# Two-layer segment-recurrent transformer on one core: the last 64 rows of the weight products as column pairs, with tiles numbered by heads

## The chip, the core and the metric

The kernel runs on one core of a Trainium2 chip. The metric is the time of one execution on the device, in microseconds. The kernel before takes 1576.67 us, the median of three runs (1576.35 to 1577.01).

## The reference, cut to what matters

Two kinds of layer alternate, twice: attention with a recurrent memory (A), and a gated feed-forward layer (B). Each is applied to a layer norm of x and added to x.

```python
scale = Dh ** (-0.5)
for s in range(n_seg):                       # 64 segments of 32 rows
    xs = x[:, s * seg_len:(s + 1) * seg_len, :]
    h = jnp.concatenate([mem, xs], axis=1)   # 8 memory rows + 32 rows, 448 wide
    q = jnp.einsum('btd,dhe->bhte', h, Wq)   # 16 heads of 256
    k = jnp.einsum('btd,dhe->bhte', h, Wk)
    v = jnp.einsum('btd,dhe->bhte', h, Wv)
    scores = jnp.einsum('bhqe,bhke->bhqk', q, k) * scale
    scores = jnp.where(mask[None, None], scores, -1000000000.0)
    p = _softmax(scores, axis=-1)
    o = jnp.einsum('bhqk,bhke->bhqe', p, v)
    o = jnp.einsum('bhte,hed->btd', o, Wo)
    mem = o[:, :M, :]                        # the next segment's memory
    outs.append(o[:, M:, :])
# B: h = relu(x @ W_gate) * (x @ W_up); x + h @ W_down
x = x + A(_layernorm(x)); x = x + B(_layernorm(x))
x = x + A(_layernorm(x)); x = x + B(_layernorm(x))
```

## The kernel before

**What is computed in which form.** The weights are multiplied first. For each head, A = Wq Wk^T (448 x 448) and B = Wv Wo (448 x 448); the scores are then h A h^T and the output is P h B. A_sb and B_sb stay on the chip for the whole run.

**Preparation (lines 289 to 435).** A loop over p = 0 to 7 makes A for two heads at a time. `load_nat` (L302) loads 512 columns of Wq and of Wk: 384 rows in one DMA, the last 64 rows in a second, and into the free half of the fourth chunk a third DMA brings 64 rows again (of Wq, or of Wv beside Wk). All of these, and first of all the rows of x (xp, L168), are issued by SyncE. `flips` (L323) turns them on TensorE with `tr` (L151), 8 transposes for each half of 256 columns, and `share` (L316) copies each result out of PSUM on VectorE or ScalarE, by a planned balance of the two. Then 8 slots (kd = 0 to 3 for the four chunks of rows, eo = 0, 1 for the two heads) multiply query rows by key rows: two matmuls of 384 columns into `aps`, and two of 64 columns into `mx_ps`. For kd = 3, the last 64 rows, the query rows stand twice, in both halves of the 128 outputs, and two copies for each head take either half. Between the slots the transposes of the next pair are placed. A second loop makes B the same way from Wv and Wo; the last 64 rows of Wv, collected in v3, are multiplied there as column pairs: two heads at a time, each in 64 columns of the array, with `tile_position` (0, 0) and (0, 64).

**Numbering.** A tile is a chunk of 128 of a head's 448 columns. A half hf holds 8 heads, and 28 tiles: tile 8 kd + 4 eo + p4 for the three full chunks, 24 + p4 for the last columns of two heads together.

**The steps (`step`, L712).** 68 steps follow; step g works on one segment of the first A layer and, from g = 4 to 63, on one of the second (60 steps with two chains; four at either end have one). In each step and half, `project` (L621) multiplies h by the tiles in banks of six (0, 6, 12, 18; and 24 with four), into PSUM. `copies` (L628) evicts each bank to TQ, where the layout is by segment part, kd and head. The 64 last rows of a tile need only half the array's rows, so `project_early` (L608) runs them ahead, two banks at a time, one on the upper and one on the lower half of the rows; EARLY (L43) says which banks go together: 0 with 6 and 12 with 18. Then `scores` (L740) takes 128 columns of TQ for each kd as weights, in the order KD = (0, 1, 3, 2): memory rows (Sm) with the first three, own rows (Sx) with the first three, then both with the last. The softmax runs on VectorE and ScalarE, and the output projection (ox, o) on TensorE.

**What sets the order.** TensorE runs its instructions in the order of the program (`in_order`, L80), in the steps VectorE and ScalarE too (`InOrder`, L93). In the preparation the order on VectorE, ScalarE, GpSimd and SyncE is what the scheduler makes of the dependencies; each of these engines then runs its list strictly in order. SyncE's DMAs use eight completion slots in turn, and a DMA that takes a slot again waits for the one that had it.

Of the kernel before, what the change touches and what calls it, by code (L numbers as in the profile page):

```python
# [8 lines left out]
BF = mybir.dt.bfloat16  # L9
# [6 lines left out]
DM = 448  # L16
# [26 lines left out]
EARLY = (((0, 6), (12, 18)), ((0, 6), (12, 18)))  # L43
# [5 lines left out]


def upper(hf, t):

    return any(b <= t < b + 6 for _, b in EARLY[hf])

# [6 lines left out]
def build_kernel(ctx, tc, A_x, A_mem0, A_Wq, A_Wk, A_Wv, A_Wo, B_W_gate, B_W_up, B_W_down, out,  # L61
# [89 lines left out]
    def tr(out, src, idn):  # L151
        in_order(nc.tensor.transpose(out, src, idn))  # L152
        passed(out, 56)
# [14 lines left out]
    nc.sync.dma_start(xp[1][:], x_dram[0:128])  # L168
# [120 lines left out]
    with tc.tile_pool(name="pre", bufs=6) as pre:  # L289
# [3 lines left out]
        nats = []  # L293
        for i in range(6):
            t = pre.tile([P, 4, 512], BF, name=f"nat{i}", bufs=1)
            nats.append(t)
        nc.gpsimd.memset(A_sb[64:128, 3, :, 24:NT, :], 0.0)
        for t in TQ + TZ + PX + PM + YB:
            nc.gpsimd.memset(t[:], 0.0)
        nn = [0]  # L300

        def load_nat(src, p, eng):  # L302
            t = nats[nn[0] % 6]
            nn[0] += 1
            cols = slice(512 * p, 512 * (p + 1))
            eng.dma_start(t[:, 0:3, :], src[0:384, cols].rearrange("(k p) n -> p k n", p=P))
            if src is Wv:
                return t
            eng.dma_start(t[0:64, 3, :], src[384:448, cols])
            eng.dma_start(t[64:128, 3, :], (Wq if src is Wq else Wv)[384:448, cols])  # L310
            return t
# [11 lines left out]
        def flips(src, p, name):  # L323
            nat = load_nat(src, p, nc.sync)
            o = pre.tile([P, 4, 512], BF, tag="tT", name=name, bufs=4)

            def half(e2):
                tp = bank([P, 2, 512], BF, "tpw")
                n = 3 if src is Wv else 4
                for kd in range(n):  # L330
                    for e in range(2):
                        tr(tp[:, e, kd * 128:(kd + 1) * 128],
                           nat[:, kd, (2 * e2 + e) * 128:(2 * e2 + e + 1) * 128], ident[:])
                n = DM if src is Wk else 128 * n
                share(o[:, 2 * e2:2 * e2 + 2, 0:n], tp[:, :, 0:n], 2 * n, (0.6, 0.82))
                if src is Wk:
                    share(v3[:, p, 2 * e2:2 * e2 + 2, :], tp[:, :, DM:512], 128, (0.6, 0.82))

            return o, [lambda: half(0), lambda: half(1)]

        def queue(p):
            if p < NP:
                qT, a = flips(Wq, p, "qT")
                kT, b = flips(Wk, p, "kT")
                return (qT, kT), a + b
            if p == NP:
                return flips(Wv, 0, "vT")
            return None, []
# [13 lines left out]
        keep_warm(8)  # L362
# [5 lines left out]

        ready, todo = queue(0)
        for k, u in enumerate(todo):  # L370
            if k == 2:
                keep_warm(4)
            u()
        for p in range(NP):
            hf, p4 = divmod(p, 4)
            qT, kT = ready
            ready, todo = queue(p + 1)
            mx_ps = bank([P, 4, 128], F32, "mxw")
            for kd in range(4):
                for eo in range(2):  # L380
                    aps = bank([P, 3, 128], F32, "aps")
                    for t in range(2):
                        e = 2 * eo + t
                        mm(aps[:, :, :], qT[:, e, kd * 128:(kd + 1) * 128],
                           kT[:, e, 0:384], start=(t == 0), stop=(t == 1))
                    for t in range(2):
                        e = 2 * eo + t
                        mm(mx_ps[:, kd, eo * 64:eo * 64 + 64], qT[:, e, kd * 128:(kd + 1) * 128],
                           kT[:, e, 384:448], start=(t == 0), stop=(t == 1))
                    t0 = eo * 4 + p4  # L390
                    if kd < 3:
                        share(A_sb[:, kd, hf, t0:t0 + 17:8, :], aps[:], 384, (1.28, 0.85))
                    else:
                        up = [t for t in range(3) if upper(hf, t0 + 8 * t)]
                        for rows, ts in ((slice(64, 128), up), (slice(0, 64), [t for t in range(3) if t not in up])):
                            if ts:
                                d = ts[1] - ts[0] if len(ts) > 1 else 1
                                share(A_sb[rows, 3, hf, t0 + 8 * ts[0]:t0 + 8 * ts[-1] + 1:8 * d, :],
                                      aps[rows, ts[0]:ts[-1] + 1:d, :], 128 * len(ts), (1.28, 0.85))
                    if todo and 2 * kd + eo in (0, 2, 4, 5):  # L400
                        todo.pop(0)()
            share(A_sb[:, 0:3, hf, 24 + p4, :], mx_ps[:, 0:3, :], 384, (1.28, 0.85))
            share(A_sb[0:64, 3, hf, 24 + p4, :], mx_ps[0:64, 3, :], 128, (1.28, 0.85))
            if p >= 5:
                load_wo(p - 5)
            if p == 1:
                xn0 = normed(row_stats(xp[1]))
            if p == 2:
                first_rows(xn0)

        for p in range(NP):
            hf, p4 = divmod(p, 4)
            vT = ready
            ready, todo = flips(Wv, p + 1, "vT") if p + 1 < NP else (None, [])
            wo = wos.pop(0)
            for eo in range(2):
                for kd in range(3):
                    bps = bank([P, 512], F32, "bps")
                    for t in range(2):
                        e = 2 * eo + t  # L420
                        mm(bps[:, 0:DM], vT[:, e, kd * 128:(kd + 1) * 128], wo[:, e, :],
                           start=(t == 0), stop=(t == 1))
                    share(B_sb[:, hf, tidx(kd, eo, p4), 0:DM], bps[:, 0:DM], DM, (1.28, 0.85))
                    if kd == 1 and todo:
                        todo.pop(0)()
            bps = bank([P, 512], F32, "bps")
            for t in range(2):
                for eo in range(2):
                    e = 2 * eo + t
                    mm(bps[64 * eo:64 * eo + 64, 0:DM], v3[:, p, e, :], wo[:, e, :],  # L430
                       start=(t == 0), stop=(t == 1), tile_position=(0, 64 * eo))
            share(B_sb[:, hf, 24 + p4, 0:DM], bps[:, 0:DM], DM, (1.28, 0.85))
            if p + 3 < NP:
                load_wo(p + 3)
            if p >= 3:
                next_piece()
                next_piece()
# [170 lines left out]
    def project_early(hf, chains, hb, j, pairs=(0, 1)):  # L608

        n = L * len(chains)  # L610
        pre = {}
        for pair in [EARLY[hf][i] for i in pairs]:
            for i0 in pair:
                pre[i0] = bank([P, 512], F32, "prj", hold=True)
            for i in range(6):
                for i0, rows in zip(pair, (slice(0, 64), slice(64, 128))):
                    mm(pre[i0][:, i * n:(i + 1) * n], A_sb[rows, 3, hf, i0 + i, :],
                       moving(hb, j, 3, chains, rows), start=(i == 0), stop=False, skip_group_check=True)
        return pre

    def project(hf, chains, hb, j, banks, pre={}, busy=False, first=None, inside=None):  # L621

        n = L * len(chains)
        for i0, k in banks:
            ps = pre[i0] if i0 in pre else bank([P, 512], F32, "prj")
            two = len(chains) == 2

            def copies(eng, rows, T):  # L628
                T = T.rearrange("p g (t q) -> p t g q", q=16)
                if two:  # L630
                    evac(eng, T, ps[rows, 0:k * n].rearrange("p (t g q) -> p t g q", t=k, q=16))
                    return
                c = chains[0]
                src = ps[rows, 0:k * n].rearrange("p (t w) -> p t w", t=k)
                x, m = (0, SEG) if c == 0 else (MEM, 0)
                evac(eng, T[:, :, 2, MEM * c:MEM * c + MEM], src[:, :, m:m + MEM])
                evac(eng, T[:, :, 3 * c:3 * c + 2, :],
                     src[:, :, x:x + SEG].rearrange("p t (g q) -> p t g q", q=16))
# [12 lines left out]
            if i0 < 24:  # L651
                T = TQ[hf][:].rearrange("p g u w -> p g (u w)")[:, :, 16 * i0:16 * (i0 + k)]
                copies(act if (i0 != 6 if busy and hf else i0 % 12) else dve, slice(0, P), T)
            else:
                copies(act if busy else dve, slice(0, 64), TZ[hf][0:64, :, 0:64])
                copies(act, slice(64, 128), TZ[hf][64:128, :, 64:128])
# [464 lines left out]
```

## Time and profile before

| what | value |
|---|---|
| median of three runs | 1576.67 us (1576.35 to 1577.01) |
| profiled execution | 1574.71 us, span 1572.9 us |
| TensorE busy in the span | 1559.8 us |
| VectorE, ScalarE, GpSimd busy | 1125.3, 744.0, 78.1 us |
| start to the first aps matmul | 9.38 us |
| first loop of the preparation | 9.38 to 48.04 us |
| second loop | 48.04 to 75.63 us |
| bytes moved by DMA | 33.21 MB, nearly all in the first three of 40 slices |

A row of the profile's groups or of its timeline names the line, the engine, the operation, what it writes and reads with shapes, how often, and its duration; in square brackets stands the idle time of the engine just before it and what ended that. Line 102 is the wrapper through which VectorE and ScalarE are called, lines 144 and 152 are the helpers for matmuls and transposes, so instructions are told apart by their tiles. PEld is TensorE's load of weights, which overlaps its matmuls. A table by stages shows for each stretch its length, then for each engine the busy time and the number of instructions, the granted clock of TensorE, the DMA engines' busy share and GB/s.

### The profile page before, as it was taken

The numbers are of one execution on the slowest core, as the hardware profiler recorded it, in microseconds if no ns is written. First come the engines' busy times: TensorE is split into PE (matmuls) and PEld (weight loads), VectorE is DVE, ScalarE is ACT, GpSimd is POOL, SyncE is SP. The second block draws the span as 40 slices with busy tenths as digits, with TensorE's granted clock in tenths as the row PEclk, the third lists the DMA queues.
The fourth block names the chain that finished last, engine by engine and source line by source line (L and its number), as shares of the span: only waits on it lengthen the run. The fifth ranks groups of instructions, "written<-read, shape, count | busy, mean of one in ns | idle before, by whom it ended". The sixth has DMA issues, their size and how long they took to land.

```text
span 1572.9 us, 89355 instructions
## 1 busy us (share of the span) xinstructions
PE 1559.8 (99%) x40988; PEld 1446.1 (92%) x40988; DVE 1125.3 (72%) x3689; ACT 744.0 (47%) x2088; POOL 78.1 (5%) x174
## 2 busy tenths in 40 slices
PE   9999999999999999999999999999999999999998
PEld 6698999999999999999999999999999999999897
DVE  7766777777777777777777777777777777777765
ACT  5754444454444444544444445444444444444443
POOL 3200000000000000000000000000000000000000
PEclk9999999999999999999999999999999999999999
DMA  8630000000000000000000000000000000000000
GB/s 242 201 85 9 8 10 9 8 5 10 9 9 9 10 9 7 7 10 9 10 9 10 10 5 8 10 10 9 10 9 10 4 10 10 9 8 7 6 7 9
DMA packets 28233, 33.21 MB, mean 21 GB/s; under 512 B 4168, under 2 KB 26960, under 8 KB 27856
## 3 DMA queue, kind: packets, MB, share of 16 engines
q1 hardware_dynamic: 26608, 23.76, 5.4%
q8 instruction: 320, 5.24, 1.4%
q0 software_dynamic: 1088, 3.68, 0.7%
q14 instruction: 57, 0.47, 0.1%
q10 hardware_dynamic: 160, 0.06, 0.0%
HBM read 23.70 MB, written 1.84 MB: 16 GB/s over the span
## 4 chain that ended last, share of the span: by engine, by line
PE 98%; DVE 1%; issue 0%; DMA 0%; SPq 0%; ACT 0%; POOLq 0%; POOL 0%; ACTq 0%; DVEq 0%
PE prj L144 32%; PE ox L144 25%; PE gps L144 6%; PE ups L144 6%; PE dps L144 5%; PE o L144 5%; PE y L144 4%; PE Sx L144 3%; PE pps L152 2%; PE bps L144 1%; PE aps L144 1%; PE Sm L144 1%; PE tpw L152 1%; PE ya L144 1%; PE yb L144 1%; PE kps L152 1%
## 5 line engine op out<-in xcount | busy, mean ns | idle before, releaser
L144 PE MATMUL prj<-hT,A_sb 128*128 128x80 bf16 (+3 forms) x15232 | 553.9, 199 | 1.0 <-DVE se L102 0.6
L144 PEld LDWEIGHTS <-A_sb 128*128 128x128 bf16 (+1 forms) x15232 | 507.3, 99 | 23.3 <-issue 1.9
L144 PEld LDWEIGHTS <-B_sb 128*128 128x128 bf16 (+1 forms) x15008 | 489.5, 103 | 14.3 <-issue 1.2
L144 PE MATMUL ox<-Y,B_sb 128*128 128x80 bf16 (+2 forms) x11256 | 443.5, 200 | 1.0 <-issue 0.8
L102 ACT CAST TQ<-prj 128x480 bf16<-128x480 f32 (+1 forms) x380 | 184.1, 496 | 116.3 <-PE prj L144 110.5
L102 DVE CAST Y<-y 128x256 bf16<-128x256 f32 x376 | 151.2, 456 | 36.5 <-PE y L144 36.2
L102 ACT CAST Y<-y 128x512 bf16<-128x512 f32 (+2 forms) x392 | 137.1, 419 | 62.4 <-PE y L144 62.3
L102 ACT ACTIVATE se<-se 128x160 f32<-128x160 f32 (+2 forms) x270 | 81.5, 302 | 140.7 <-DVE se L102 135.4
L102 DVE CAST TQ<-prj 128x480 bf16<-128x480 f32 (+1 forms) x228 | 128.4, 572 | 9.0 <-PE prj L144 8.5
L144 PE MATMUL gps<-xT,Wg_sb 128*128 128x128 bf16 (+3 forms) x1904 | 128.6, 215 | 0.0
L144 PEld LDWEIGHTS <-Wu_sb 128*128 128x128 bf16 (+1 forms) x1904 | 104.9, 97 | 5.7 <-issue 0.2
L144 PEld LDWEIGHTS <-hk 40*128 40x128 bf16 (+1 forms) x1950 | 98.9, 96 | 9.8 <-issue 2.7
L144 PE MATMUL ups<-xT,Wu_sb 128*128 128x128 bf16 (+3 forms) x1632 | 106.8, 216 | 0.5 <-DVE xT L102 0.5
L144 PEld LDWEIGHTS <-Wg_sb 128*128 128x128 bf16 (+1 forms) x1904 | 106.7, 97 | 0.5 <-issue 0.5
L102 ACT COPY os<-o 64x16 f32<-64x16 f32 (+3 forms) x134 | 25.5, 190 | 172.3 <-PE o L144 170.8
L102 ACT CAST TZ<-prj 64x320 bf16<-64x320 f32 (+2 forms) x264 | 96.9, 377 | 17.1 <-DVE TZ L102 13.6
L102 DVE SCALAR_TENSOR_TENSOR hh<-gps,ut 128x512 bf16<-128x512 f32 (+2 forms) x136 | 78.0, 594 | 34.6 <-ACT ut L102 21.8
L144 PE MATMUL dps<-Wd_sb,hh 128*128 128x448 bf16 (+1 forms) x504 | 93.3, 342 | 0.8 <-DVE hh L102 0.8
L102 DVE TENSOR_REDUCE ssum<-se 128x4 f32<-128x160 f32 (+2 forms) x270 | 72.7, 269 | 24.1 <-ACT se L102 24.0
L102 ACT COPY PT<-pps 128x256 bf16<-128x256 bf16 (+1 forms) x136 | 46.5, 343 | 91.0 <-PE pps L152 90.9
L144 PEld LDWEIGHTS <-TQ 128*128 128x128 bf16 x1938 | 85.9, 97 | 1.6 <-ACT TQ L102 0.8
L144 PE MATMUL y<-PT,hk 40*128 40x256 bf16 (+1 forms) x1280 | 86.3, 248 | 0.7 <-ACT Y L102 0.6
(127 smaller groups left out, 1901.6 us busy)
## 6 DMA issues: line engine op xcount, KB each, us to landing
wo<-in_A_Wo_dram POOLq DMA_DIRECT2D x8, 448.0 KB, 5.1
nat<-in_A_Wq_dram SPq DMA_DIRECT2D x8, 384.0 KB, 4.9
nat<-in_A_Wk_dram SPq DMA_DIRECT2D x8, 384.0 KB, 4.8
nat<-in_A_Wv_dram SPq DMA_DIRECT2D x8, 384.0 KB, 4.7
xa<-in_A_x_dram SPq DMA_DIRECT2D x32, 56.0 KB, 2.2
xa<-xp SPq DMA_DIRECT2D x32, 56.0 KB, 1.9
xp<-in_A_x_dram SPq DMA_DIRECT2D x30, 56.0 KB, 2.7
out_dram<-xa SPq DMA_DIRECT2D x30, 56.0 KB, 2.5
```

Of the source, the lines that this page charges most:

```text
L102: r = f(*a, **k)
L144: in_order(nc.tensor.matmul(out, lhsT, rhs, **k))
L152: in_order(nc.tensor.transpose(out, src, idn))
```

## The change

What it does:

- The last 64 rows of Wq and of Wk are loaded into the two halves of one tile (natl), turned together in 4 transposes, and multiplied as column pairs (`by_heads`, `last_rows`): two heads at a time, 64 rows each, 448 columns. The chunk kd = 3 leaves the loop of slots, which has 6 slots a pair. The last rows of Wv are loaded for two pairs of heads at a time and turned in the second loop.
- `last_rows` and `last_out` stand at the end of an even pair and at the start of an odd one, so that two groups are adjacent.
- The first pair's loads are split by heads (256 columns each) and issued by SyncE (Wq) and ScalarE (Wk), ahead of everything else; the first loads go at the top of the program. The load of xp moves into the loop, behind the loads of the second pair.
- The first pair's second head is turned inside the loop; the junk matmuls that keep TensorE busy (`keep_warm`) are 7, 2 and 2 instead of 8 and 4.
- Tiles are numbered by heads: tile 3 (4 eo + p4) + kd. EARLY pairs bank 0 with 12 and 6 with 18, and `copies` writes TQ with one dimension more.

The core of the diff:

```diff
-EARLY = (((0, 6), (12, 18)), ((0, 6), (12, 18)))
+EARLY = ((0, 12), (6, 18))
...
-    nc.sync.dma_start(xp[1][:], x_dram[0:128])
+    prepare = ExitStack()
+    pre = prepare.enter_context(tc.tile_pool(name="pre", bufs=6))
+    nats = [pre.tile([P, 3, 512], BF, name=f"nat{i}", bufs=1) for i in range(6)]
+    nats3 = [pre.tile([P, 512], BF, name=f"natl{i}", bufs=1) for i in range(3)]
...
+    for e in range(2):
+        cols = slice(256 * e, 256 * e + 256)
+        for i, (eng, src) in enumerate(((nc.sync, Wq), (nc.scalar, Wk))):
+            eng.dma_start(nats[i][:, :, cols], rows3(src, cols))
+            if e == 0:
+                eng.dma_start(nats3[0][FR[i], :], src[384:448, 0:512])
...
+        def flip(nat, e2, dst):
+            tp = bank([P, 2, 512], BF, "tpw")
+            for kd in range(3):
+                for e in range(2):
+                    tr(tp[:, e, kd * 128:(kd + 1) * 128],
+                       nat[:, kd, (2 * e2 + e) * 128:(2 * e2 + e + 1) * 128], ident[:])
+            share(dst, tp[:, :, 0:384], 768, (0.6, 0.82))
+
+        def flip_last(nat, dst):
+            tp = bank([P, 4, 128], BF, "tpl")
+            for e in range(4):
+                tr(tp[:, e, :], nat[:, e * 128:e * 128 + 128], ident[:])
+            share(dst, tp[:].rearrange("p e (i d) -> p e i d", i=2), 512, (0.6, 0.82))
...
-        keep_warm(8)
+        keep_warm(7)
...
+        def by_heads(ps, a, b, n):
+            for t in range(2):
+                for eo in range(2):
+                    mm(ps[FR[eo], 0:n], a(2 * eo + t), b(2 * eo + t), start=(t == 0), stop=(t == 1),
+                       tile_position=(0, 64 * eo))
+
+        def last_rows(qk, hf, p4):
+
+            ps = bank([P, DM], F32, "apl")
+            by_heads(ps, lambda e: qk[:, e, 0, 384:DM], lambda e: qk[:, e, 1, :], DM)
+            for eo in range(2):
+                t0 = 3 * (eo * 4 + p4)
+                share(A_sb[FR[eo], 3, hf, t0:t0 + 3, :], ps[FR[eo], 0:384], 384, (1.28, 0.85))
+            for eo in range(2):
+                share(A_sb[FR[eo], 3, hf, 24 + p4, 64 * eo:64 * eo + 64], ps[FR[eo], 384:DM], 64, (1.28, 0.85))
+
         ready, todo = queue(0)
-        for k, u in enumerate(todo):
-            if k == 2:
-                keep_warm(4)
-            u()
+        for k in range(3):
+            todo.pop(0)()
+            if k < 2:
+                keep_warm(2)
         for p in range(NP):
             hf, p4 = divmod(p, 4)
-            qT, kT = ready
-            ready, todo = queue(p + 1)
-            mx_ps = bank([P, 4, 128], F32, "mxw")
-            for kd in range(4):
-                for eo in range(2):
+            qk = ready
+            ready, us = queue(p + 1)
+            todo += us
+            if p == 0:
+                nc.sync.dma_start(xp[1][:], x_dram[0:128])
+            if p % 2:
+                last_rows(qk, hf, p4)
+            mx_ps = bank([P, 3, 128], F32, "mxw")
+            for eo in range(2):
+                t0 = 3 * (eo * 4 + p4)
+                for kd in range(3):
...
-                    if kd < 3:
-                        share(A_sb[:, kd, hf, t0:t0 + 17:8, :], aps[:], 384, (1.28, 0.85))
...
+                    share(A_sb[:, kd, hf, t0:t0 + 3, :], aps[:], 384, (1.28, 0.85))
+                    if todo:
                         todo.pop(0)()
...
+            while todo:
+                todo.pop(0)()
+            if p % 2 == 0:
+                last_rows(qk, hf, p4)
...
-                T = T.rearrange("p g (t q) -> p t g q", q=16)
+                l = T.shape[1]
                 if two:
-                    evac(eng, T, ps[rows, 0:k * n].rearrange("p (t g q) -> p t g q", t=k, q=16))
+                    evac(eng, T, ps[rows, 0:k * n].rearrange("p (l t g q) -> p l t g q", l=l, g=5, q=16))
...
-                T = TQ[hf][:].rearrange("p g u w -> p g (u w)")[:, :, 16 * i0:16 * (i0 + k)]
+                T = TQ[hf][:].rearrange("p g u w -> p g (u w)").rearrange("p g (t m q) -> p m t g q", t=3, q=16)
+                T = T[:, i0 // 3:i0 // 3 + 2]
```

The last two lines select for a bank the two heads i0 / 3 and i0 / 3 + 1, with all three kd each, and write them to the places that they had in TQ before. Loading, turning and multiplying the same rows gives the same A and B as before.

More of the change, by code (lines that the diff above doesn't have):

```diff
@@ L48 @@
 HALF = (slice(0, DM // 2), slice(DM // 2, DM))
-def upper(hf, t):
-    return any(b <= t < b + 6 for _, b in EARLY[hf])
 def tidx(kd, eo, p4):
@@ L166, in block, with rows3 @@
         return slice(TB * i, TB * i + TB)
-    nc.sync.dma_start(xp[1][:], x_dram[0:128])
+    prepare = ExitStack()
+    pre = prepare.enter_context(tc.tile_pool(name="pre", bufs=6))
+    nats = [pre.tile([P, 3, 512], BF, name=f"nat{i}", bufs=1) for i in range(6)]
+    nats3 = [pre.tile([P, 512], BF, name=f"natl{i}", bufs=1) for i in range(3)]
+    def rows3(src, cols):
+        return src[0:384, cols].rearrange("(k p) n -> p k n", p=P)
+    for e in range(2):
[4 more added lines that the diff above has]
+                eng.dma_start(nats3[0][FR[i], :], src[384:448, 0:512])
     still = glob.tile([P, 512], BF, name="still")
@@ L286, in set_mem @@
         dve.tensor_copy(mem_of(g, cs)[:, 0:src.shape[1]], src)
-    with tc.tile_pool(name="pre", bufs=6) as pre:
+    with prepare:
         mem0_n = pre.tile([MEM, 512], BF, name="mem0_n", bufs=1)
@@ L292, in build_kernel, with load_nat, load_last @@
         nc.gpsimd.dma_start(mem0_n[:, DM:512], mem0[:, 384:DM])
[L293 to L297, printed above, removed]
+        for e in range(2):
+            nc.gpsimd.memset(A_sb[FR[e], 3, :, 24:NT, 64 - 64 * e:128 - 64 * e], 0.0)
         for t in TQ + TZ + PX + PM + YB:
             nc.gpsimd.memset(t[:], 0.0)
-        nn = [0]
-        def load_nat(src, p, eng):
+        nn, n3 = [2], [1]
+        def load_nat(src, p):
             t = nats[nn[0] % 6]
             nn[0] += 1
[L305 to L310, printed above, removed]
+            nc.sync.dma_start(t[:], rows3(src, slice(512 * p, 512 * p + 512)))
+            return t
+        def load_last(parts):
+            t = nats3[n3[0] % 3]
+            n3[0] += 1
+            for r, (src, p) in zip(FR, parts):
+                nc.sync.dma_start(t[r, :], src[384:448, 512 * p:512 * p + 512])
             return t
@@ L321, in share @@
             evac(eng, dst, src)
[L323 to L339, printed above, removed]
+        def flip(nat, e2, dst):
+            tp = bank([P, 2, 512], BF, "tpw")
+            for kd in range(3):
+                for e in range(2):
+                    tr(tp[:, e, kd * 128:(kd + 1) * 128],
+                       nat[:, kd, (2 * e2 + e) * 128:(2 * e2 + e + 1) * 128], ident[:])
+            share(dst, tp[:, :, 0:384], 768, (0.6, 0.82))
@@ L341, in queue @@
+        def flip_last(nat, dst):
[3 more added lines that the diff above has]
+            share(dst, tp[:].rearrange("p e (i d) -> p e i d", i=2), 512, (0.6, 0.82))
         def queue(p):
             if p < NP:
[L343 to L347, printed above, removed]
@@ L348, in queue @@
-            return None, []
+                nat = nats[0:2] if p == 0 else [load_nat(src, p) for src in (Wq, Wk)]
+                last = nats3[0] if p == 0 else load_last(((Wq, p), (Wk, p)))
+                qk = pre.tile([P, 4, 2, DM], BF, tag="qk", name="qk", bufs=2)
+                us = [lambda i=i, e2=e2: flip(nat[i], e2, qk[:, 2 * e2:2 * e2 + 2, i, 0:384])
+                      for e2 in range(2) for i in range(2)]
+                us.insert(2, lambda: flip_last(last, qk[:, :, :, 384:DM]))
@@ new lines, in queue, with queue_v @@
+                return qk, us
+            return queue_v(p - NP)
+        def queue_v(p):
+            us = []
+            if p % 2 == 0:
+                last = load_last(((Wv, p), (Wv, p + 1)))
+                us.append(lambda: flip_last(last, v3[:, p:p + 2].rearrange("p a e d -> p e a d")))
+            nat = load_nat(Wv, p)
+            vT = pre.tile([P, 4, 384], BF, tag="vT", name="vT", bufs=2)
+            return vT, us + [lambda e2=e2: flip(nat, e2, vT[:, 2 * e2:2 * e2 + 2, :]) for e2 in range(2)]
@@ L381, in build_kernel @@
                     aps = bank([P, 3, 128], F32, "aps")
                     for t in range(2):
-                        e = 2 * eo + t
-                        mm(aps[:, :, :], qT[:, e, kd * 128:(kd + 1) * 128],
-                           kT[:, e, 0:384], start=(t == 0), stop=(t == 1))
+                        mm(aps[:, :, :], qk[:, 2 * eo + t, 0, kd * 128:(kd + 1) * 128],
+                           qk[:, 2 * eo + t, 1, 0:384], start=(t == 0), stop=(t == 1))
                     for t in range(2):
-                        e = 2 * eo + t
@@ L388, in build_kernel @@
-                        mm(mx_ps[:, kd, eo * 64:eo * 64 + 64], qT[:, e, kd * 128:(kd + 1) * 128],
-                           kT[:, e, 384:448], start=(t == 0), stop=(t == 1))
-                    t0 = eo * 4 + p4
-                    if kd < 3:
-                        share(A_sb[:, kd, hf, t0:t0 + 17:8, :], aps[:], 384, (1.28, 0.85))
[L393 to L399, printed above, removed]
@@ L400, in build_kernel @@
-                    if todo and 2 * kd + eo in (0, 2, 4, 5):
-                        todo.pop(0)()
-            share(A_sb[:, 0:3, hf, 24 + p4, :], mx_ps[:, 0:3, :], 384, (1.28, 0.85))
-            share(A_sb[0:64, 3, hf, 24 + p4, :], mx_ps[0:64, 3, :], 128, (1.28, 0.85))
+                        mm(mx_ps[:, kd, eo * 64:eo * 64 + 64], qk[:, 2 * eo + t, 0, kd * 128:(kd + 1) * 128],
+                           qk[:, 2 * eo + t, 1, 384:DM], start=(t == 0), stop=(t == 1))
+                    share(A_sb[:, kd, hf, t0:t0 + 3, :], aps[:], 384, (1.28, 0.85))
@@ L404, in build_kernel @@
+                    if todo:
+                        todo.pop(0)()
+            share(A_sb[:, 0:3, hf, 24 + p4, :], mx_ps[:], 384, (1.28, 0.85))
+            while todo:
+                todo.pop(0)()
+            if p % 2 == 0:
+                last_rows(qk, hf, p4)
             if p >= 5:
@@ L409, in build_kernel, with last_out @@
                 first_rows(xn0)
+        def last_out(p, wo):
+            ps = bank([P, 512], F32, "bps")
+            by_heads(ps, lambda e: v3[:, p, e, :], lambda e: wo[:, e, :], DM)
+            hf, p4 = divmod(p, 4)
+            share(B_sb[:, hf, 24 + p4, 0:DM], ps[:, 0:DM], DM, (1.28, 0.85))
         for p in range(NP):
@@ L413, in build_kernel @@
             vT = ready
-            ready, todo = flips(Wv, p + 1, "vT") if p + 1 < NP else (None, [])
+            ready, todo = queue_v(p + 1) if p + 1 < NP else (None, [])
             wo = wos.pop(0)
+            if p % 2:
+                last_out(p, wo)
             for eo in range(2):
@@ L423, in build_kernel @@
                     share(B_sb[:, hf, tidx(kd, eo, p4), 0:DM], bps[:, 0:DM], DM, (1.28, 0.85))
-                    if kd == 1 and todo:
+                    if kd < 2 and todo:
                         todo.pop(0)()
[L426 to L432, printed above, removed]
+            if p % 2 == 0:
+                last_out(p, wo)
             if p + 3 < NP:
@@ L611, in project_early @@
         pre = {}
-        for pair in [EARLY[hf][i] for i in pairs]:
+        for pair in [EARLY[i] for i in pairs]:
             for i0 in pair:
@@ L628, in copies @@
             def copies(eng, rows, T):
-                T = T.rearrange("p g (t q) -> p t g q", q=16)
+                l = T.shape[1]
                 if two:
-                    evac(eng, T, ps[rows, 0:k * n].rearrange("p (t g q) -> p t g q", t=k, q=16))
+                    evac(eng, T, ps[rows, 0:k * n].rearrange("p (l t g q) -> p l t g q", l=l, g=5, q=16))
                     return
                 c = chains[0]
-                src = ps[rows, 0:k * n].rearrange("p (t w) -> p t w", t=k)
+                src = ps[rows, 0:k * n].rearrange("p (l t w) -> p l t w", l=l, w=n)
                 x, m = (0, SEG) if c == 0 else (MEM, 0)
-                evac(eng, T[:, :, 2, MEM * c:MEM * c + MEM], src[:, :, m:m + MEM])
-                evac(eng, T[:, :, 3 * c:3 * c + 2, :],
-                     src[:, :, x:x + SEG].rearrange("p t (g q) -> p t g q", q=16))
+                evac(eng, T[:, :, :, 2, MEM * c:MEM * c + MEM], src[:, :, :, m:m + MEM])
+                evac(eng, T[:, :, :, 3 * c:3 * c + 2, :],
+                     src[:, :, :, x:x + SEG].rearrange("p l t (g q) -> p l t g q", q=16))
             for i in range(k):
@@ L651, in project @@
             if i0 < 24:
-                T = TQ[hf][:].rearrange("p g u w -> p g (u w)")[:, :, 16 * i0:16 * (i0 + k)]
+                T = TQ[hf][:].rearrange("p g u w -> p g (u w)").rearrange("p g (t m q) -> p m t g q", t=3, q=16)
+                T = T[:, i0 // 3:i0 // 3 + 2]
                 copies(act if (i0 != 6 if busy and hf else i0 % 12) else dve, slice(0, P), T)
             else:
-                copies(act if busy else dve, slice(0, 64), TZ[hf][0:64, :, 0:64])
-                copies(act, slice(64, 128), TZ[hf][64:128, :, 64:128])
+                for eng, e in ((act if busy else dve, 0), (act, 1)):
+                    T = TZ[hf][FR[e], :, 64 * e:64 * e + 64].rearrange("p g (m q) -> p m g q", q=16)
+                    copies(eng, FR[e], T.unsqueeze(1))
             if i0 in (6, 18):
```

## The prediction

> **What bounds the kernel now.** Read first, on the page, the busy times and the 40 slices: TensorE is busy almost everywhere, so only what changes TensorE's own work, or makes it wait, is worth time. The table by stages comes second; its two long stages are the preparation's first half and the 60 steps with two chains.
>
> ```profile
> PE 1559.8 (99%) x40988; PEld 1446.1 (92%) x40988; DVE 1125.3 (72%) x3689; ACT 744.0 (47%) x2088; POOL 78.1 (5%) x174
> ...
> 9.40:48.04 38.64, 38.52 (x501) 29.89 (x501) 34.85 (x76) 24.62 (x69) 7.45 (x14) 1.00 0.88 266
> ...
> 148.00:1471.00 1323.00, 1321.27 (x35180) 1247.00 (x35176) 957.70 (x3151) 619.68 (x1681) 46.56 (x118) 1.00 0.03 9
> ```
>
> The reader should see that the steps (1323 us) leave TensorE idle for under 2 us. Nothing there can absorb a new wait: a wait on TensorE lengthens the kernel by its own length, 60 times over. The change is named for the preparation, but renumbering the tiles reaches into every step; so I look third at the timeline of one step with feed-forward work, on ScalarE and TensorE.
>
> ```profile
> 794.48 0.56 ACT L102 CAST TQ<-prj 128x480 bf16<-128x480 f32 x1 [0.37 <-PE prj L144]
> ...
> 794.83 0.13 PEld L144 LDWEIGHTS <-TQ 128*128 128x128 bf16 x2
> ...
> 795.24 0.21 PEld L144 LDWEIGHTS <-TQ 128*128 128x128 bf16 x5
> ```
>
> The cast evicts bank 18, the last of the second half's projections, and ends at 795.04. The scores of that half load their first weights from TQ at 794.83, before it ends. That is allowed, because in the old numbering (tile = 8 kd + head) bank 18 holds only kd = 2, which the order KD = (0, 1, 3, 2) reads last, at 795.24. I look fourth at the start of the kernel, on VectorE and SyncE.
>
> ```profile
> 0.73 0.39 SPq L168 DMA_DIRECT2D xp<-in_A_x_dram  x1
> ...
> 2.80 0.63 DVE L102 BATCH_NORM_STATS2 stats<-xp 128x6 f32<-128x448 bf16 x1 [1.57 <-DMA xp<-in_A_x_dram]
> ...
> 4.75 0.15 DVE L102 TENSOR_SCALAR blk<-blk 128x1 f32<-128x1 f32 x1
> ...
> 5.89 1.29 DVE L102 COPY qT<-tpw 128x1024 bf16<-128x1024 bf16 x2 [0.99 <-PE tpw L152]
> ...
> 8.70 1.16 DVE L102 COPY kT<-tpw 128x896 bf16<-128x896 bf16 x2 [1.52 <-PE tpw L152]
> ```
>
> VectorE runs the statistics of the first rows before any weight eviction, and waits for xp's DMA to do so. That is cheap now, since xp is SyncE's first issue.
>
> **Main loop: a wait moves forward.** In the new numbering (tile = 3 head + kd) every bank holds two heads with all three kd, so the first weights (kd = 0) need bank 18 too. The built program agrees: the wait for ScalarE before kd = 2 is gone and stands at the first load of these scores. ScalarE cannot start earlier: it idles 0.37 us before the cast, waiting for the bank's matmuls. Over all 60 steps with two chains the cast ends after the first score matmul by 0.13 us in one kind of step (821.58 against 821.45) and 0.19 in the other (795.04 against 794.85); the sum is 9.9 us. A waiting TensorE starts 0.05 us after ScalarE's end:
>
> ```profile
> 171.00 0.52 ACT L102 COPY PT<-pps 128x128 bf16<-128x128 bf16 x2
> ...
> 171.30 0.27 PE L144 MATMUL ya<-PT,hk 128*128 128x128 bf16 x2 [0.75 <-ACT PT L102]
> ```
>
> (The second of the two copies takes 0.25 us and ends at 171.25.) So 9.9 + 60 x 0.055 = **13.2 us**, 0.22 a step. Everything behind it on TensorE is queued: the other scores, then the output projection. The softmax chains start later by the same amount as their consumers, so they give nothing back. The first half's scores run 0.98 us after their own cast (817.10 to 818.08), and stay clear. The new casts write four dimensions where they wrote three; Y's casts of 128x512 already do, at 585 ns on ScalarE against TQ's 558 for 480 columns, the same time per column, so nothing. In the 8 steps with one chain a cast comes in two parts and TensorE already waits for the first (0.2 us in some), so I take 0, bounds 0 and 1 us.
>
> **Preparation: TensorE's work.** Before, a pair costs 32 transposes x 0.056 + 8 slots x 0.382 (two 384-column matmuls at 0.162, two of 64 at 0.028) = 4.85 us; the chain shows 4.86. After: 28 x 0.056 + 6 x 0.382 + one group of four 64-column matmuls. The nearest row is bps<-v at 50.91, which takes 0.60 us with the changes of shape around it; two groups adjacent save one change, so 0.50 each. That makes 4.36. Over the loop, with the first pair's 12 transposes left and 16 for the first value pair: 18.3 + 12.5 + 4.0 + 0.75 (first rows, as now) = 35.6 against 38.7. The second loop gains 0.8 from adjacent groups and pays 12 transposes (0.7). Sum **-3.2 us**. Evictions fall with the work, about 3.7 us a pair and engine under 4.36, so they stay hidden on average; but a group that opens an odd pair needs the eviction of a transpose made 0.5 to 0.9 us before, which takes 0.2 + 0.56 + 0.06: I take **+0.7** of short waits (bounds 0 and 2).
>
> **Preparation: the first eviction.** Here the moved load counts. xp's issue goes from SyncE's first to its eighth (it waits for a landed slot too), behind 786 KB of the first pair, 786 KB of the second and 131 KB of last rows. In VectorE's order as built, the statistics still stand ahead of the first eviction. With xp, 1.95 MB must have moved; the windows of 1 us show 1.98 MB by 10.0 us. A steady 305 GB/s from 2 us on would give 8.4; half speed for the first pair's shorter rows about 11.5. I take 9.7. From statistics to the end of the setup is 2.0 us (2.80 to 4.90, less two instructions now ahead), then two evictions of 768 columns at 0.55 (from 0.68 for 1024 and 0.62 for 896): first aps at 9.7 + 2.0 + 1.1 + 0.05 = 12.85, not 9.38: **+3.5**, and 0.1 for the last rows' eviction that mx needs. TensorE stands idle from about 6.7 to 12.85. At the span's start it is slow: 427 ns for a junk matmul, 215 after 5.75 us. Whether six idle us bring that back no row shows; bounds 0 and 2.3 us (half of 4.57). I take **+2.0**, since the start is the one place where it begins after long idleness.
> The Trainium skill, "TensorE: Matmul & The Clock Gate", section "Part 1: The HAM clock gate", says that the clock falls to half after an idle window of about 3.4 us and needs about as long a busy one to return. By it the term would be about 1.7 us, and without it the sum is 2.0 lower; it speaks against a change that idles TensorE here, and no run yet shows it.
>
> **Sum.** 13.2 - 3.2 + 0.7 + 3.6 + 2.0 = +16.3 us. The profiled execution took 1574.7 us (span 1572.9 and 1.8 around it), giving 1591.0; the median shown is 1576.7, 2.0 higher, so I forecast **1593 us**.
>
> **Rivals.** *VectorE is not held* (xp lands by 5 us, or the queues drain quicker than these windows): the junk matmuls and cold transposes put the first aps with its mx near 7.0, so -2.4 - 3.2 + 0.7 = -4.9, and with the steps' wait 1585. For it: two queues issue at once where SyncE spends 0.4 to 0.6 us on each. Against it: the eight issues and the bytes ahead of xp. *The casts get longer* in the new layout, by 0.1 us: 60 x 0.1 more, 1599; Y's row speaks against it. *The wait is hidden*, VectorE held: 1576.7 + 3.1 = 1580, about no change. *Faster*: the steps' wait vanishes because the cast ends before the first weights are due, and the preparation gains its 4.9: 1572. It decides at 4.9 / 60 = 0.08 us a step; the idle 0.37 before the cast says that ScalarE has no way to be so much earlier.
>
> **How the numbers follow.** Forecast 0.62, VectorE free 0.18, longer casts 0.10, hidden wait 0.05, faster 0.05. A measurement of this kernel can tell about 0.2%, 3.2 us, from no change. Slower: the first three and half of the fourth, 0.92; same 0.04; faster 0.04. The bounds (xp -1.3 and +1.8, clock -2.0 and +0.3, short waits -0.7 and +1.3, single chains +1) and the two rivals next to the forecast ask for 1583 to 1599.
>
> **What would show it.** Right: an idle of some 0.2 us before the LDWEIGHTS of TQ, released by ScalarE's TQ, 60 times; the statistics waiting for xp until about 10 us; the first aps near 12.9; slow matmuls after it; the stage 148 to 1471 longer by 13. Wrong: no such idle, or qk evicted before 7 us. A time under 1580 would refute the main step.

## The result, and the profile after

| kernel | median | profiled: span | preparation ends | from there to the end |
|---|---|---|---|---|
| before, same chip | 1576.84 us (1576.35 to 1578.56, 4 runs) | 1572.9 | 75.56 | 1497.3 |
| after | 1595.58 us (1593.66 to 1596.79, 4 runs) | 1591.8 | 82.85 | 1508.9 |

The changed kernel is slower: ratio 1.0118, 95% interval 1.0106 to 1.013. "Preparation ends" is the start of the first projection matmul of the steps. Of the 18.9 us that the span grew, the preparation holds 7.3 and the steps 11.6; the prediction had 3.1 and 13.2, 16.3 in all.

The page of the changed kernel, busy times, then the first line of the chain (shares of the span by engine):

```profile
PE 1566.9 (98%) x40939; PEld 1446.7 (91%) x40939; DVE 1123.9 (71%) x3685; ACT 746.1 (47%) x2080; POOL 78.2 (5%) x175
...
PE 96%; DVE 1%; ACT 1%; DMA 1%; issue 0%; SPq 0%; POOL 0%; POOLq 0%; ACTq 0%; DVEq 0%
```

TensorE still looks busy all the time: its share fell by one point, its busy time even grew by 7.1 us with 49 instructions fewer. The busy times don't show the loss. The chain gives the first hint: ScalarE and DMAs, at 0% before, now hold 1% each. Which rows these are, the table of the weight loader's waits tells (us in total, times, longest; the last row is the kernel before):

```profile
PEld L139 <- DVE qk L97: 8.3, 1, 8.3
PEld L139 <- ACT TQ L97: 7.5, 37, 0.3
...
PEld L144 <- ACT TQ L102: 0.8, 4, 0.2
```

Both rows of the changed kernel are new in size: the wait on ScalarE's TQ was 0.8 us in 4 cases, and before the first aps matmul TensorE had waited 0.27 us, for kT. One step shows the wait itself, on ScalarE and TensorE (start, duration, engine, line, operation, idle before):

```profile
807.70 0.56 ACT L97 CAST TQ<-prj 128x480 bf16<-128x480 f32 x1 [0.36 <-PE prj L139]
...
807.96 0.28 PE L139 MATMUL yb<-PT,hk 128*128 128x128 bf16 x3
...
808.31 0.11 PEld L139 LDWEIGHTS <-TQ 128*128 128x128 bf16 x2 [0.20 <-ACT TQ L97]
808.31 0.25 PE L139 MATMUL Sm<-hT,TQ 128*128 128x80 bf16 x2
```

The cast of bank 18 ends at 808.26 and the scores' first weights load 0.05 us later, after 0.20 us of idleness. Before, the same load stood ahead of the cast's end. TensorE's own rows hide most of the wait: the yb matmuls ahead of it count as busy until 808.24, 0.07 us before the Sm matmuls start. The start of the kernel is the other place, VectorE first, then TensorE:

```profile
11.05 0.63 DVE L97 BATCH_NORM_STATS2 stats<-xp 128x6 f32<-128x448 bf16 x1 [9.70 <-DMA xp<-in_A_x_dram]
11.60 1.77 DVE L97 CAST rowf<-rowi 128x3 f32<-128x3 int32 x1
11.66 1.73 DVE L97 CAST keyf<-keyi 128x32 f32<-128x32 int32 x1
11.74 1.65 DVE L97 BATCH_NORM_AGGREGATE mv<-stats 128x2 f32<-128x6 f32 x1
...
14.20 1.01 DVE L97 COPY qk<-tpw 128x768 bf16<-128x768 bf16 x2
```

```profile
6.34 0.39 PE L147 MATMUL tpl<-ident,natl 128*128 128x128 bf16 x4
15.27 0.80 PE L139 MATMUL aps<-qk 128*128 128x384 bf16 x2 [8.54 <-DVE qk L97]
15.86 0.31 PE L139 MATMUL mxw<-qk 128*128 128x64 bf16 x2
15.98 0.83 PE L147 MATMUL tpw<-ident,nat 128*128 128x128 bf16 x6
```

VectorE waits for xp until 11.05, then for something that holds three small operations for 1.7 us each, and evicts the first transposes at 14.20. TensorE is idle for 8.54 us and then slow: two aps matmuls take 0.80 us here and 0.49 from 19.17 on. The table of stretches gives the granted clock in its last column but two (stretch, length, busy PE, PEld, DVE, ACT, POOL, clock, DMA share, GB/s):

```profile
6.80:15.20 8.40, 0.00 (x0) 0.10 (x1) 4.13 (x14) 0.00 (x0) 8.23 (x14) 0.82 0.84 226
15.30:18.80 3.50, 3.50 (x25) 2.47 (x25) 1.36 (x3) 0.96 (x2) 0.23 (x1) 0.50 0.21 58
19.00:22.00 3.00, 3.00 (x44) 2.40 (x43) 2.13 (x5) 2.17 (x5) 0.00 (x0) 1.00 0.55 179
```

### The profile page after: what moved, and what is told of

Same layout as the page of the kernel before. It is cut to its first block, busy times and chain, and to the rows that moved or that the text cites. A ratio compares the mean times of both kernels' runs of the same rounds, so it can differ in the third digit from the quotient of the medians.

```text
span 1591.8 us, 89240 instructions
## 1 busy us (share of the span) xinstructions
PE 1566.9 (98%) x40939; PEld 1446.7 (91%) x40939; DVE 1123.9 (71%) x3685; ACT 746.1 (47%) x2080; POOL 78.2 (5%) x175
## 4 chain that ended last, share of the span: by engine, by line
PE 96%; DVE 1%; ACT 1%; DMA 1%; issue 0%; SPq 0%; POOL 0%; POOLq 0%; ACTq 0%; DVEq 0%
PE prj L139 32%; PE ox L139 25%; PE gps L139 6%; PE ups L139 6%; PE dps L139 5%; PE o L139 5%; PE y L139 4%; PE Sx L139 2%; PE Sm L139 2%; PE pps L147 1%; PE bps L139 1%; ACT TQ L97 1%; PE aps L139 1%; PE kps L147 1%; PE tps L147 1%; PE tpw L147 1%
```

## The experiments

Theory: two costs that add and have nothing to do with each other. In the steps, the second half's scores read bank 18's result at once instead of last, so TensorE waits for a cast that it used to run beside. In the preparation, the moved load of xp holds VectorE, and with it the first evictions. Rivals: the numbering, the EARLY order or the new casts cost something of their own; the preparation's late end is just more waiting on loads.

Each kernel was timed beside the kernel before on its chip (medians 1575.65, 1574.90 and 1575.35 us for runs 1 to 4, 5 to 8 and 9 to 11). The last two columns split the growth of the profiled span, one execution of each kernel, at the preparation's end (us).

| run | median, ratio (95%) | preparation | steps |
|---|---|---|---|
| 1 before, kd = 2 read first | 1587.78, 1.0079 (1.0064 to 1.0094) | +0.1 | +12.7 |
| 2 before, new numbering only | 1588.09, 1.0081 (1.0066 to 1.0097) | -0.1 | +13.2 |
| 3 after, xp loaded first | 1585.53, 1.0064 (1.0047 to 1.0081) | -1.5 | +12.5 |
| 4 after, bank 18 evicted by two engines | 1608.72, 1.0210 (1.0195 to 1.0226) | +7.2 | +26.6 |
| 5 after, bank 24 last | 1592.88, 1.0116 (1.0102 to 1.0130) | +6.9 | +11.0 |
| 6 runs 3 and 5 together | 1584.94, 1.0066 (1.0054 to 1.0079) | -1.7 | +11.9 |
| 7 run 6, last rows at their own pair | 1583.23, 1.0056 (1.0043 to 1.0070) | -2.8 | +10.2 |
| 8 after, Y's memset later | 1594.16, one run | +7.6 | +11.8 |
| 9 after, old numbering | 1582.33, 1.0046 (1.0032 to 1.0061) | +9.4 | -1.8 |
| 10 run 9, xp first, last rows at their own pair | 1574.91, 0.9994 (0.9985 to 1.0003) | +1.7 | -0.9 |
| 11 after, junk matmuls in the idle time | 1593.37, one run | +6.5 | +12.1 |

### 1 and 2: the wait alone, made in two ways

Run 1 changes one line of the kernel before; nothing else of the change is in it:

```diff
-KD = (0, 1, 3, 2)
+KD = (2, 0, 1, 3)
```

> The kernel before with one line changed, KD = (2, 0, 1, 3): the scores read kd = 2 first, the chunk that bank 18 holds in the old numbering. Nothing of the preparation, of the numbering or of the copies is changed. Theory (the steps are longer because the first weights of the second half's scores need bank 18): an idle of 0.14 to 0.20 us before that load of weights, 60 times, and the time of before plus 11 to 13 us, about 1588. Rival (the steps are longer because of the new write pattern of the copies or of the banks that EARLY pairs): no idle, and the time of before within 0.2%.

Run 2 is the kernel before with the numbering, EARLY and `copies` of the changed kernel:

```diff
-EARLY = (((0, 6), (12, 18)), ((0, 6), (12, 18)))
+EARLY = ((0, 12), (6, 18))
...
-                    t0 = eo * 4 + p4
+                    t0 = 3 * (eo * 4 + p4)
```

> The kernel before with the new numbering alone: tile 3 head + kd, EARLY pairing 0 with 12 and 6 with 18, and the copies of the changed kernel. The preparation keeps its loads, its transposes and its eight slots; two copies of the last rows for each pair of heads become one of the same total size. Theory: plus 11 to 13 us against before, about 1588, all of it between the first step and the last, and a preparation that ends at 75.6 us as before. Rival (the renumbered tiles cost nothing and the whole loss is the preparation's): the time of before within 0.2%.

The two cost the same. Over 48 steps with two chains, which take 1081.40 us before, both grow by 10.09 us, and the passage from the last yb matmul to the first Sm grows from 1.38 to 12.02 us in both. Run 1's waits show the row of the changed kernel:

```profile
PEld L144 <- ACT TQ L102: 7.8, 37, 0.5
```

So the order of reading is enough to make the cost, and the numbering brings nothing else to the steps: its EARLY order and its casts are free (the ScalarE row of TQ is 496 ns on average before and after, VectorE's 572 and 573). The rival of longer casts falls.

### 3: xp loaded first

```diff
+    nc.sync.dma_start(xp[1][:], x_dram[0:128])
...
-            if p == 0:
-                nc.sync.dma_start(xp[1][:], x_dram[0:128])
```

> The changed kernel with the load of xp put back as SyncE's first issue. Theory (VectorE's order puts the statistics of xp ahead of the first eviction, and xp lands late): the statistics start near 2.8 us, the first aps matmul comes near 7 to 7.5 us in place of 15.27, the matmuls after it run at full speed from the start, and the time falls by 8 (the late start) plus 1.8 (the slow matmuls), to about 1586. Rival (the first weights' loads or TensorE's transposes set the start): the first aps stays above 12 us and the time falls by less than 3 us.

```profile
3.29 0.63 DVE L97 BATCH_NORM_STATS2 stats<-xp 128x6 f32<-128x448 bf16 x1 [2.07 <-DMA xp<-in_A_x_dram]
...
5.57 0.56 DVE L97 COPY qk<-tpw 128x768 bf16<-128x768 bf16 x1
```

The preparation ends 8.8 us sooner than in the changed kernel, the first aps start at 7.52, and no slow stretch follows. Moving that one load costs 8.8 us of the 18.9. But the preparation is only 1.5 us ahead of the kernel before, though its first aps start 1.9 us earlier and TensorE has some 3.1 us less to do: about 3.5 us of short waits take the rest. (A short wait is counted as the time by which a matmul starts later behind the one ahead of it than the same succession of matmuls does elsewhere.)

### 4: a shorter eviction of bank 18, tried

```diff
+                if two and hf and i0 == 18:
+                    for m, eng in ((0, dve), (1, act)):
+                        evac(eng, T[:, m], ps[:, 3 * n * m:3 * n * m + 3 * n].rearrange("p (t g q) -> p t g q", t=3, q=16))
+                else:
```

> The changed kernel with bank 18 of the second half, in steps with two chains, evicted by VectorE (one head) and ScalarE (the other) in place of ScalarE alone. Theory: the later half's copy takes about 0.36 us for 240 columns in place of 0.56, so the wait before the load of TQ falls from 0.14 and 0.20 to about 0.00 and 0.05, and the time falls by 9 to 11 us, to about 1585. Rival (the wait is not what the steps lose): the time stays within 0.2% of the changed kernel.

This missed: 14 us slower than the changed kernel, each against the kernel before on its chip. VectorE, ScalarE and the weight loader in one step:

```profile
842.59 0.41 DVE L97 CAST TQ<-prj 128x240 bf16<-128x240 f32 x1
...
843.03 0.36 ACT L97 CAST TQ<-prj 128x240 bf16<-128x240 f32 x1 [0.58 <-DVE TQ L97]
...
843.44 0.11 PEld L139 LDWEIGHTS <-TQ 128*128 128x128 bf16 x2 [0.39 <-ACT TQ L97]
```

The program makes ScalarE wait for VectorE's half, so two casts of 240 columns, 0.41 and 0.36 us, follow one another and end later than one of 480 (0.56). The premise of the run, two halves at once, didn't hold. What it shows is the theory with the other sign: the later the bank's end, the longer the kernel. The wait between yb and Sm grew to 23.35 us in 48 steps.

### 5, 6 and 7: a bank that is needed late goes last

Bank 24 (kd = 3) is projected last and read last, half of it evicted by VectorE:

```diff
-BANKS = (((0, 6), (6, 6), (24, 4), (12, 6), (18, 6)), ((0, 6), (24, 4), (6, 6), (12, 6), (18, 6)))
+BANKS = (((0, 6), (6, 6), (24, 4), (12, 6), (18, 6)), ((0, 6), (6, 6), (12, 6), (18, 6), (24, 4)))
...
-KD = (0, 1, 3, 2)
+KD = (0, 1, 2, 3)
...
-                for eng, e in ((act if busy else dve, 0), (act, 1)):
+                for eng, e in ((act if busy and not (two and hf) else dve, 0), (act, 1)):
```

> The changed kernel with another order of the second half's banks: 0, 6, 12, 18 and then 24 (kd = 3, evicted to TZ by VectorE and ScalarE, half each), and KD = (0, 1, 2, 3), so that the chunk of the last bank is read last. The numbering by heads, the copies and the preparation stay. Theory: bank 18's cast now ends before the first weights of the second half's scores are due, the 60 idles before the load of TQ vanish, and the time falls by 11 to 12 us, to about 1584. Rival (the steps lose time to the numbering itself): the time stays within 0.2% of the changed kernel's 1595.6.

Run 6 adds the edit of run 3.

> Both repairs: xp first on SyncE, and the banks and KD of the kernel with bank 24 last. Theory (two separate losses that add up): the 1585.5 of the kernel with xp first less 11 to 12, that is 1573 to 1575, at or a little under the 1575.7 of before. Rival (the losses overlap, or the preparation's work costs as much as before): above 1578.

Both missed: the wait at TQ is gone and a new one stands at TZ. Run 6, one step:

```profile
824.75 0.48 DVE L97 CAST TZ<-prj 64x320 bf16<-64x320 f32 x1
...
825.14 0.49 PEld L139 LDWEIGHTS <-TQ 128*128 128x128 bf16 x15
...
825.26 0.42 ACT L97 CAST TZ<-prj 64x320 bf16<-64x320 f32 x1 [0.59 <-DVE TZ L97]
...
825.73 0.20 PEld L139 LDWEIGHTS <-TZ 128*128 128x128 bf16 x5
```

The scores now load TQ without a pause at 825.14, fifteen times, and then stop for TZ until 825.73. Bank 24 is evicted in two casts of 64 partitions, which again run one after the other, so its eviction takes 0.93 us from the start of the first, not 0.56. Putting the late bank last helps only if its eviction is as short as the reading that covers it.

Run 7 is run 6 with `last_rows` at the end of each pair instead of two groups side by side:

```diff
-            if p % 2:
-                last_rows(qk, hf, p4)
...
-            if p % 2 == 0:
-                last_rows(qk, hf, p4)
+            last_rows(qk, hf, p4)
```

> The kernel with both repairs, and each pair's last rows multiplied at the end of its own pair, in place of two groups next to each other at the turn from an even to an odd pair. Theory (the short waits of 3.8 us in the preparation's first loop come from two groups' eight evictions at once, behind which the transposes' evictions stand): these waits fall to about 1 us, each group costs 0.1 us more for its changes of shape, and the time falls by about 2 us against both repairs. Rival (the waits come from the total of the evictions): the time stays or rises by 0.8 us.

The preparation gains 1.1 us and the median 1.7: with the groups apart, the short waits of the first loop fall from 3.1 to 1.0 us, and the long one behind two groups, which an eviction of ScalarE ended, is gone. Against that stand about 0.8 us more of TensorE's own work (an estimate: the first loop less its short waits is 36.3 us in run 7 and 35.5 in run 6).

### 8: what held VectorE's three small operations

The memset of the first Y moves behind GpSimd's part of the statistics:

```diff
-        for t in TQ + TZ + PX + PM + YB:
+        for t in TQ + TZ + PX + PM:
...
+    nc.gpsimd.memset(YB[0][:], 0.0)
```

> The changed kernel with GpSimd's memset of the first Y moved from 11.4 us to behind its part of the statistics. Theory (VectorE's conversions of the row and key numbers and its aggregate, 1.65 to 1.77 us each from 11.6 us on, wait until GpSimd's memset of Y is over at 13.34 us): each takes 0.17 to 0.18 us, the setup ends 1.0 to 1.6 us earlier and the first aps matmul comes at 13.7 to 14.3 us in place of 15.27. Rival (they are slow because of the late statistics or of their own operands): they stay at 1.7 us.

GpSimd in the changed kernel, then VectorE in run 8:

```profile
11.38 1.96 POOL L304 MEMSET Y<- 128x2240 bf16 x1
```

```profile
11.45 0.15 DVE L97 CAST rowf<-rowi 128x3 f32<-128x3 int32 x1
11.51 0.17 DVE L97 CAST keyf<-keyi 128x32 f32<-128x32 int32 x1
11.59 0.17 DVE L97 BATCH_NORM_AGGREGATE mv<-stats 128x2 f32<-128x6 f32 x1
```

The memset ended at 13.34, and so, within 0.06 us, did the three operations. Without it they take 0.15 to 0.17 us, and the first aps start at 13.52, not 15.27. The Trainium skill, "SBUF — State Buffer", section "SBUF: two separate sides", says that VectorE and GpSimd share a pair of ports, which one instruction (of VectorE's only some, by mode and inputs) holds for its whole length. The trace agrees in that; which mode these three ran in no run shows. In the kernel before the aggregate took 0.18 us beside GpSimd's memset of hT, so here it may only have stood in line behind the two casts. The gain didn't reach the end: the clock stayed at half for 5.6 us of TensorE's work, not 3.7, which takes back 0.9; the second loop then waited 1.0 us for wo; and the preparation ended no sooner.

### 9 and 10: the preparation alone

Run 9 is the changed kernel with the old numbering. The halves of EARLY then need the last rows of each head in two places, so a group's tiles take four evictions instead of two:

```diff
-EARLY = ((0, 12), (6, 18))
+EARLY = (((0, 6), (12, 18)), ((0, 6), (12, 18)))
...
-                t0 = 3 * (eo * 4 + p4)
-                share(A_sb[FR[eo], 3, hf, t0:t0 + 3, :], ps[FR[eo], 0:384], 384, (1.28, 0.85))
+                t0 = eo * 4 + p4
+                up = [t for t in range(3) if upper(hf, t0 + 8 * t)]
+                for rows, ts in ((FR[1], up), (FR[0], [t for t in range(3) if t not in up])):
...
```

> The changed kernel with the old numbering of the tiles put back, in the preparation's copies and in the main loop, so that only the preparation's part of the change is left: column-pair groups for the last 64 rows, query and key rows turned together, first loads by heads on two queues, rows of x loaded late. Theory (two separate costs that add: a wait of TensorE in the steps that belongs to the numbering, and a late start that belongs to the moved load of x): no idle before the second half's scores; the preparation ends 7 to 8 us later than before, as in the changed kernel; 1574.9 + 7.3 = about 1582, bounds 1580 to 1585 (four evictions of the last rows a pair in place of two). Rival (the new preparation also costs something in the steps, by where it leaves the banks or the weights): above 1586. Rival (the late start is absorbed once the steps do not wait): under 1578.

Run 10 adds the edits of runs 3 and 7.

> The run before with x's rows loaded first, as in the kernel before, and the groups of the last rows at the end of their own pair: the part of the change that should be a gain by itself. Theory: the preparation ends 1.5 to 3 us earlier than before, the steps are as before, so 1572 to 1574, 0.1 to 0.2% faster than before, at the edge of what the measurement can tell. Rival (the added evictions of the last rows in the old numbering, four a pair in place of two, hold TensorE in the first loop): 1575 to 1578, no gain.

In run 9 the distance to the kernel before stays between 8.9 and 9.0 us from step 4 to step 54: the steps cost nothing, and 1.8 come back at their two ends. So the costs add: by the spans, run 9's 7.6 and run 2's 13.1 make 20.7, less the 2.1 by which run 9's preparation is later than the changed kernel's (1.1 of them the clock, at half for 5.8 us here), 18.6; measured 18.9.

Run 10 came out as its rival said: no gain (the interval holds 1). Its first aps start at 8.42, a microsecond before those of the kernel before, but its preparation ends 1.7 later. TensorE's waits in it:

```profile
PE aps L144 <- ACT A_sb L102: 1.4, 2, 0.7
PE aps L144 <- DVE A_sb L102: 0.9, 2, 0.7
```

In run 7, with two evictions of 384 columns a group, this list holds 0.2 us of such waits; all short waits of the loops sum to about 1.1 us there and 4.4 here. The numbering by heads is thus what makes the column pairs cheap to evict, worth about 3.3 us in the preparation, and it costs 12.7 to 13.2 in the steps. (The two preparations lie 4.5 us apart, +1.7 against -2.8; the other 1.3 are a first aps 0.6 us later and a clock that came to full speed later, which the numbering doesn't touch.) No version tried beats the kernel before by more than can be measured.

### 11: TensorE kept busy

```diff
-            if k < 2:
-                keep_warm(2)
+            keep_warm(2 if k < 2 else 36)
```

> The changed kernel with 36 matmuls of zeros put behind the third transposed unit, so that TensorE is not idle while it waits for the first eviction. Theory (the slow matmuls after the wait come from the idle time itself): transposes at 56 ns and aps at 162 ns from the first of them on, the preparation's end 1.5 to 2 us earlier than in the changed kernel, if the matmuls of zeros end before the first eviction does. Rival (the clock is low because of the time since the start of the execution): the same slow rows until about 19 us. The time of one look tells nothing here.

The first aps start at 15.28, as in the changed kernel (15.27), but at the full clock, here in the stretches of run 11:

```profile
6.10:14.00 7.90, 7.90 (x40) 3.46 (x37) 2.60 (x9) 0.00 (x0) 7.67 (x12) 1.00 0.94 266
15.30:18.80 3.50, 3.50 (x47) 2.79 (x47) 2.80 (x7) 1.94 (x5) 0.25 (x1) 1.00 0.27 70
```

In the same 3.5 us TensorE runs 47 instructions, not 25: the idle time made it slow, not the time since the start. The Trainium skill, "TensorE: Matmul & The Clock Gate", section "Part 1: The HAM clock gate", gives half speed after an idle window of about 3.4 us and as long a busy one to return. The traces agree in the half, 0.50, and in the order of size: it lasted 3.7 us of work in the changed kernel (15.27 to 18.93), 2.8 in run 5, 5.6 in run 8 and 5.8 in run 9. A pause of 1.21 us in run 11 didn't bring it. At 23.3 us run 11 is 1.64 us ahead of the changed kernel; of that, 0.8 reach the preparation's end, since wo is then waited for (0.7).

## Why the prediction was right, point by point

- **The steps' wait: right.** Predicted 13.2, measured 11.6 (11.8 to 12.5 in runs 3, 8 and 11, whose steps are the same), and runs 1 and 2 make it alone. The release 0.05 us after the cast is as predicted. A step loses 0.216 us between yb and Sm (0.22 predicted) and gets 0.009 back in its scores, for a reason that no run shows; over 60 steps that makes 12.4, and the other 0.8 come back outside these stretches, which no run takes apart. A caution on reading: the table of waits shows 7.5 us in 37 cases, not 12 in 60. It counts the weight loader's idleness only, and leaves out the gaps of 0.14 us that every other step has; the timeline has to be summed step by step.
- **Late xp: right in that VectorE waits for it, too small, and the memset of run 8 was left out.** Predicted +3.5 for the first aps, measured +5.9 (15.27 against 9.38). By the sum xp landed at 11.03, not 9.7, and from the statistics to the first eviction took 3.15 us, not 2.0; the 2.0 is from the kernel before, where the two casts came behind GpSimd's memset. But the landing wasn't what set the time. In runs 4, 5, 9 and 11 xp landed at 11.4 to 12.2 us, and the first aps still started at 15.26 to 15.28, because in each the three operations ended with the memset, at 13.36 to 13.41. Run 9's VectorE (the changed kernel's evicts at 14.20 too):

```profile
12.24 0.63 DVE L102 BATCH_NORM_STATS2 stats<-xp 128x6 f32<-128x448 bf16 x1 [10.89 <-DMA xp<-in_A_x_dram]
...
14.20 1.01 DVE L102 COPY qk<-tpw 128x768 bf16<-128x768 bf16 x2
```

- **Slow clock: right**, 1.8 for 2.0 (the 3.7 us at half speed), and its cause is shown by run 11. That it came so close is partly luck: with the same first aps the half speed lasted from 2.8 us (run 5) to 5.8 (run 9), a cost of 1.4 to 2.9.
- **TensorE's work: as predicted.** The first loop takes 40.0 us from its first aps to the first bps; less 1.8 for the clock and 2.7 of short waits that is 35.5 (35.6 predicted). The apl groups take 4.08 us (4.0), 0.4 of it a wait. The second loop is 0.1 us shorter: its matmuls take 0.8 less and its transposes 0.7 more, as summed. The -3.2 as a whole is what remains: 7.3 less 5.9, 1.8 and 2.7 of short waits is -3.1.
- **Short waits: outside the bounds.** Predicted 0.7, at most 2; measured 2.7. The largest, seen at 24.96 to 26.46, isn't the one that was priced (a transpose's eviction ahead of an odd pair's group), but one behind the two groups: their evictions queue on both engines, and the next aps wait for a bank.

```profile
26.46 0.49 PE L139 MATMUL aps<-qk 128*128 128x384 bf16 x2 [1.28 <-ACT A_sb L97]
```

- **Rivals.** VectorE not held: refuted by 9.70 us of waiting. Longer casts: refuted by the row of TQ. Hidden wait, and faster: refuted by runs 1 and 2.

The median lies 2.6 us over the forecast because the preparation's errors (+2.4, -0.2 and +2.0) outweigh the steps' (-1.6).

## What to carry to other kernels

A renumbering is a change of order: list for each consumer which producer it reads first and which last, since the last producer's eviction is hidden only as long as its result is read last. A load that is moved back takes with it all that stands behind its consumer on that engine, here the first evictions, and a TensorE that was idle for 8.5 us is slow afterwards as well. Work saved on the bounding engine is worth only what the engines behind it can evict: of the 3.1 us saved here, 1.2 were left from the first aps to the preparation's end with the groups apart (run 7), and none with two groups side by side (run 3).

## What the runs showed of the hardware that was not expected

- Small operations of VectorE between buffers in SBUF (128x3, 128x32) took 1.73 to 1.77 us beside GpSimd's memset of 128x2240 and 0.15 to 0.17 without. They ended when the memset did, whenever they had started. Evictions from PSUM beside the same memset in the kernel before were not held:

```profile
11.40 0.56 DVE L102 CAST A_sb<-aps 128x384 bf16<-128x384 f32 x1
```

- Half the columns take well over half the time in an eviction: 240 columns take 0.41 us on VectorE and 0.36 on ScalarE, 480 take 0.65 and 0.56.
- The clock fell within an idle time of 8.5 us, about 5.4 us after the last matmul (6.73 us); in run 8, after the same work, about 2.0 us after it (6.79). The estimate is from the granted clock of single microseconds, 1.00 before these and 0.50 behind them, first in the changed kernel, then in run 8:

```profile
12.00:13.00 1.00, 0.00 (x0) 0.00 (x0) 1.00 (x3) 0.00 (x0) 1.00 (x1) 0.55 0.88 172
...
8.00:9.00 1.00, 0.00 (x0) 0.00 (x0) 0.00 (x0) 0.00 (x0) 1.00 (x1) 0.91 1.10 286
```
